# Moving the query pass behind the key and value passes, and writing the last round of a Strassen down-projection in a fixed order on all engines

## The chip, the cores and the metric

The kernel runs on one core of one Trainium2 chip. The metric is the device time of one execution in microseconds; the median of several executions is compared.

## The reference

The input x has 2048 tokens of 1024 values. All arithmetic is fp32.

```python
xn = _layernorm(x)
q, k, v = split_heads(xn @ wqkv)               # 32 heads of 32
phi(p) = concat(softmax(p), softmax(-p))       # p = q @ w_phi or k @ w_phi, per head
kv = einsum("bhsf,bhsd->bhfd", phi(pk), v);  z = sum over s of phi(pk)
s = (phi(pq) @ kv / (phi(pq) @ z + 1e-6)) @ wo
gate, up = xn @ w1, xn @ w3                    # 1024 -> 3584
g = silu((silu(gate) * up) @ w2)               # 3584 -> 1024
return x + s * g
```

## The kernel before, in words

Every large product is one level of a Strassen-like scheme with seven products (`ORDER`): operand sums are formed by VectorE, each fp32 operand is split into a high and a low fp32r part (`split`: a cast on ScalarE, a subtraction on VectorE), and three matmuls (`PASSES`) stand for one. The seven results go to three PSUM banks `a`, `b` and `c`. A bank takes several of the products one after another, so a product that adds to a bank waits until the bank's earlier value has been copied out. The stages run in this order.

1. **Gate and up** (`gate_up`, matmuls at L598): it leaves the hidden values in `h_d` in HBM, and the split operands of later stages in `xo_d`, `wkv_d` and `w2_d`.
2. **Three passes over the tokens** (loop `for c in range(3)` at L977). A pass takes eight pairs of token tiles; a pair is a block of seven products of twelve matmuls. Before the change, pass 0 is the query pass (`query_heads`, matmuls at L858), passes 1 and 2 are the key and value passes for the two halves of the heads (`heads`, L794, with the small `kv` products at L779). Each block loads the next pair's seven operands (`reload`, L563), 512 KB each. During a pass the next pass's seven weight operands of 2 MB are fetched (`fetch`, L167). The key and value passes split `wo` too (`wo_split`). The last pass also loads the first down operands (`load_b`).
3. **Query features** (`query_features`): of each of the four 128x512 quarters of a block, VectorE takes maximum and minimum (L837, L838), GpSimd, or VectorE for the last quarter, subtracts them (L839, L840), ScalarE takes the exponential (L842), and ScalarE's queue issues the DMA to `e_d` (L847). The quarters stand in two rooms of a pool `rw` with two buffers. Before, both rooms were taken once (`e_rooms`): room 0 had quarters (0,0) and (0,1), room 1 had (1,1) and (1,0). The quarters become ready in the order (0,0), (1,1), (0,1), (1,0), after the products A12, S3, S4 and A22. The key pass takes its rooms from the same pool (`room_ev`).
4. **Down** (`product`, L1135): seven rounds `kb` of eight pairs `i`, in steps. A step does three products of a new pair (`FIRST`) and four of the pair before, six matmuls each (`TURN`). `a_first` and `a_second` load the hidden values of a pair and prepare them; ScalarE, GpSimd and VectorE add results to 16 slabs in SBUF. In the last round finished slabs go through `gate` (Silu, L1035, and a store to `g_d`, L1036), and become the place of the attention's features. `load_kvz` and `load_e` (L1077) bring in what the attention needs, and `pieces` holds the first three tiles' normalisation (`z_products` on GpSimd, `z_sums` on VectorE, `weigh`, a small matmul in `add_pairs`, `invert`, `factors`, `scale`, `turn_e`), each at a pair and a place in the step.
5. **Attention and output** (from L1228): for each of 16 token tiles, `attend` (L1251), two halves of 24 matmuls (`out_half`, L1266), `gated` and a store. The weights come by `load_wo` (L1030), the gates by `load_g` (L1237).

Where `in_order(...)` names engines, their instructions stand in the order in which the code writes them; otherwise a scheduler puts each engine's instructions in an order of its own. Before, down's rounds leave all engines to the scheduler from step 6 on, and from the last half step on (`new is None`) SP, ScalarE, VectorE and GpSimd follow the written order. SP issues all DMAs but those to `e_d`, in order, and holds the ones behind a DMA that has to wait. A new DMA takes one of eight semaphores and waits until that semaphore's last DMA has landed.

## Time and profile before

| | us |
|---|---|
| median of 3 runs (lowest, highest) | 2419.08 (2416.06, 2419.09) |
| the profiled execution's own time | 2423.55 |
| its span from first to last instruction | 2421.8 |
| TensorE busy in the span | 2366.6 |
| VectorE, ScalarE, GpSimd busy | 1770.9, 856.9, 253.4 |

The busy time of TensorE counts its matmuls from start to end, and they overlap, so a busy share near one says little. What counts here is the distance from one matmul's start to the next, and the places where it grows. The mean granted clock of TensorE is 0.994 of full speed.

### The profile page before, as it was taken

To read this page: it belongs to the slowest core of one execution; us is meant where nothing else is said; L and a number is where in the kernel's file an instruction comes from. 1 tells how busy PE (TensorE), PEld (TensorE's weight loads), DVE (VectorE), ACT (ScalarE), POOL (GpSimd) and SP (SyncE) were. 2 spreads that over 40 slices of the span, in tenths; PEclk is the share of its full clock that TensorE was granted. 3 is DMA by queue.
4 is the path that set the end of the run, shared out by engine and by line. 5 is a ranking of instruction groups with operands and counts; after the bars stand their busy time and mean duration, and the time that the engine had idled before them with its cause. 6 is when DMAs were issued, how large, how long until landed. Compare 5 with 4: busy or idle time off the path is not lost.

```text
span 2421.8 us, 37223 instructions
## 1 busy us (share of the span) xinstructions
PE 2366.6 (98%) x14354; PEld 1941.1 (80%) x14354; DVE 1770.9 (73%) x2779; ACT 856.9 (35%) x1501; POOL 253.4 (10%) x249
## 2 busy tenths in 40 slices
PE   7999999999999999999998999999999999988999
PEld 6888888888888888888777888888888888766887
DVE  8877787765688888864676666666678888785775
ACT  6445454443455455442222222224322222231000
POOL 1000000000000000000331000000011111133662
PEclk9999999999999999999999999999999999999999
DMA  5446799976887988756999868855443244459773
GB/s 211 148 161 207 249 351 337 328 251 206 285 291 273 313 275 309 265 215 239 373 354 340 307 216 327 291 165 208 174 174 137 99 174 181 128 167 296 198 206 118
DMA packets 290001, 578.00 MB, mean 239 GB/s; under 512 B 24464, under 2 KB 140320, under 8 KB 287136
## 3 DMA queue, kind: packets, MB, share of 16 engines
q1 hardware_dynamic: 285216, 558.85, 67.8%
q10 hardware_dynamic: 4608, 16.78, 1.7%
q8 instruction: 113, 1.85, 0.3%
q14 instruction: 64, 0.52, 0.1%
HBM read 370.54 MB, written 205.00 MB: 238 GB/s over the span
## 4 chain that ended last, share of the span: by engine, by line
PE 46%; DMA 4%; DVE 1%; ACT 0%; issue 0%; SPq 0%; ACTq 0%
PE bankb L1135 12%; PE bankb L794 7%; PE pm L1266 7%; PE bankc L1135 6%; PE bankc L794 4%; PE banka L1135 3%; PE bankb L858 2%; PE banka L794 2%; DMA xoS<-xo_d1S 2%; PE bankc L858 1%; PE pkv L779 1%; PE po L1251 1%; DMA acc<-e_d 1%; DMA g_d<-acc 1%; PE banka L858 0%; DMA wos<-wo_d 0%
## 5 line engine op out<-in xcount | busy, mean ns | idle before, releaser
L93 DVE TENSOR_TENSOR bo<-rw,bo 128x512 fp32r<-128x512 f32 x336 | 230.9, 689 | 158.0 <-ACT bo L92 155.3
L92 ACT CAST bo<-rw 128x512 fp32r<-128x512 f32 x336 | 206.5, 617 | 12.9 <-DMA w_d2B<-w2o 3.1
L1135 PE MATMUL bankb<-bo,as 128*128 128x512 f32 x816 | 200.9, 389 | 0.0
L1135 PEld LDWEIGHTS bankb<-bo,as 128*128 128x128 f32 x816 | 153.2, 188 | 31.8
L598 PE MATMUL bankb<-op0S,bo 128*128 128x512 f32 x672 | 163.0, 391 | 1.9 <-ACT op0S L92 1.2
L598 PE MATMUL bankc<-op0S,bo 128*128 128x512 f32 x672 | 162.5, 391 | 0.3 <-DVE op0S L93 0.3
L598 PE MATMUL bankb<-op1S,bo 128*128 128x512 f32 x672 | 161.4, 389 | 0.9 <-ACT u L633 0.9
L598 PE MATMUL bankc<-op1S,bo 128*128 128x512 f32 x672 | 161.5, 389 | 0.0
L598 PE MATMUL bankb<-op0A,bo 128*128 128x512 f32 x672 | 159.7, 391 | 0.8 <-DVE bo L93 0.5
L598 PE MATMUL bankb<-op1A,bo 128*128 128x512 f32 x672 | 157.7, 390 | 0.0
L839 POOL TENSOR_TENSOR eq<-q,mm 128x512 f32<-128x512 f32 x24 | 25.3, 1052 | 1209.7 <-DVE mm L837 1113.7
L1135 PE MATMUL bankc<-bo,as 128*128 128x512 f32 x576 | 148.9, 393 | 1.5 <-ACT as L92 1.2
L1266 PE MATMUL pm<-wos,oT 128*128 128x512 f32 x576 | 141.5, 398 | 8.9 <-DVE oT L1257 6.0
L598 PEld LDWEIGHTS bankb<-op0S,bo 128*128 128x128 f32 x672 | 125.2, 188 | 28.5 <-ACT op0S L92 1.6
L598 PEld LDWEIGHTS bankb<-op1S,bo 128*128 128x128 f32 x672 | 126.0, 188 | 27.5 <-ACT u L633 1.3
L598 PEld LDWEIGHTS bankb<-op1A,bo 128*128 128x128 f32 x672 | 125.9, 188 | 27.4 <-DVE u L641 1.3
L598 PEld LDWEIGHTS bankc<-op1S,bo 128*128 128x128 f32 x672 | 126.1, 188 | 26.5 <-DVE bo L93 0.3
L598 PEld LDWEIGHTS bankb<-op0A,bo 128*128 128x128 f32 x672 | 125.2, 188 | 26.9 <-DVE bo L93 0.8
L598 PEld LDWEIGHTS bankc<-op0S,bo 128*128 128x128 f32 x672 | 125.3, 188 | 26.3 <-DVE op0S L93 0.7
L1266 PEld LDWEIGHTS pm<-wos,oT 128*128 128x128 f32 x576 | 108.0, 190 | 34.8 <-DVE oT L1257 6.8
L1135 PEld LDWEIGHTS bankc<-bo,as 128*128 128x128 f32 x576 | 108.4, 189 | 26.0 <-ACT as L92 2.2
L1147 DVE TENSOR_TENSOR acc<-bankb,acc 128x512 f32<-128x512 f32 x152 | 104.1, 686 | 26.7 <-PE bankb L1135 19.3
(249 smaller groups left out, 4412.6 us busy)
## 6 DMA issues: line engine op xcount, KB each, us to landing
rw<-in_w SPq DMA_DIRECT2D x112, 512.0 KB, 4.5
hr<-h_d SPq DMA_DIRECT2D x56, 512.0 KB, 3.6
h_d<-h SPq DMA_DIRECT2D x111, 256.0 KB, 4.9
xoS<-xo_d0S SPq DMA_DIRECT2D x44, 512.0 KB, 5.6
xoS<-xo_d1S SPq DMA_DIRECT2D x44, 512.0 KB, 5.2
xoA<-xo_d0A SPq DMA_DIRECT2D x33, 512.0 KB, 5.9
xoA<-xo_d1A SPq DMA_DIRECT2D x33, 512.0 KB, 5.4
e_d<-eq ACTq DMA_DIRECT2D x32, 512.0 KB, 7.7
```

The costliest lines, as they stand in the source:

```text
L92: nc.scalar.copy(hi, src)
L93: (by or nc.vector).tensor_sub(lo, src, hi.bitcast(F))
L598: nc.tensor.matmul(bank[b], bos[tb, f][bn][:, w, k], ao[an][:, u, k], start=first and n == 0, stop=LAST[b] == an and n == 11, skip_group_c ...
L779: nc.tensor.matmul(pkv[sl, m], e[:, m // 4, (m % 4) * P + 32 * h:(m % 4) * P + 32 * h + 32], v[:, 4 * (m % 4) + h], start=first and m == 0 ...
L794: nc.tensor.matmul(bank[b], xo[an][:, u, k], wb[bn][:, w, k], start=an in ("A11", "A12", "S1") and n == 0, stop=LAST[b] == an and n == 11, ...
L839: eng.tensor_sub(e[:, 0], p3, mm[:, 0, :].unsqueeze(2).to_broadcast([P, 16, DH]))
L858: nc.tensor.matmul(bank[b], xo[an][:, u, k], wb[bn][:, w, k], start=an in ("A11", "A12", "S1") and n == 0, stop=LAST[b] == an and n == 11, ...
L1135: nc.tensor.matmul(bank[b], t[:, u, pos + k], bos[kb, bn, k][:, w], start=first and n == 0, stop=LAST[b] == an and n == 5, skip_group_chec ...
L1147: nc.vector.tensor_add(c, pb, c)
L1251: nc.tensor.matmul(po[32 * j:32 * j + 32, a, 64 * k:64 * k + 64], kvs[sl, j, c, k], et[sl, :, 4 * k + j], start=True, stop=True, skip_grou ...
L1266: nc.tensor.matmul(p, oTs[t, h][:, a, k], wos[c, 4 * h + k][:, b], start=n == 0, stop=n == 3 * ND - 1)
```

## The change

The query pass becomes the third pass. Pass 0 and 1 are the key and value passes of the two halves, and the pending `kv` product and the first stores of `kv_out` move into the query pass's first block. The two rooms are no longer held for the whole pass. Each block takes an "early" room for quarters (0,0) and (1,1), and a "late" room for (0,1) and (1,0), from the same pool of two buffers.

In down's last round all five engines follow the written order from the round's first pair on. The operand preparation is cut into parts that stand between the products (`first_parts`, `second_parts`), the hidden values are loaded two pairs ahead, a pair's two gates come two steps after its first products instead of one, one in the middle of each half of the step, and the pieces of the normalisation have new places. The first tile's features get two ring slots of their own (`e0`) instead of slabs, and are loaded at the round's start. The order in which pairs use the slabs changes, and so do the places at which `wo` is loaded.

```diff
-            nc.sync.dma_start(t.bitcast(F), wkv_d[m - 2][n])
+            nc.sync.dma_start(t.bitcast(F), wkv_d[(1, 2, 0)[m - 2]][n])
...
+        def e_room():
+            return rwp.tile([P, 2, D], F, name="eq", tag="rw")
...
             elif an == "A12":
                 nc.vector.tensor_add(q00, pb, q00)
-                query_features(i, 0, 0, q00, rho, nc.gpsimd)
+                early = e_room()
+                query_features(i, 0, 0, q00, rho, nc.gpsimd, early[:, 0])
             elif an == "S3":
                 nc.vector.tensor_add(q11, pb, q11)
-                query_features(i, 1, 1, q11, rho, nc.gpsimd)
+                query_features(i, 1, 1, q11, rho, nc.gpsimd, early[:, 1])
             elif an == "S4":
                 nc.vector.tensor_add(q01, pb, q01)
-                query_features(i, 0, 1, q01, rho, nc.gpsimd)
+                late = e_room()
+                query_features(i, 0, 1, q01, rho, nc.gpsimd, late[:, 0])
             else:
-                query_features(i, 1, 0, pb, rho, nc.vector)
+                query_features(i, 1, 0, pb, rho, nc.vector, late[:, 1])
...
+            if an == "S1" and first:
+                kv(*pend)
+                out_now.extend(kv_out(1, pkv))
...
-            if c:
-                pend = heads(pos == 0, end, xo, wb, steps(), pend)
+            if last:
+                query_heads(i, pos == 0, xo, wb, steps())
             else:
-                query_heads(i, xo, wb, steps())
+                pend = heads(pos == 0, end, xo, wb, steps(), pend)
...
     pieces = {
-        (3, 0): [lambda: z_products(0)],
...
-        (8, 0): [lambda: z_sums(2, 1)],
+        (1, 5): [lambda: z_products(0)],
+        (2, 5): [lambda: z_sums(0, 0)],
+        (2, 6): [lambda: z_sums(0, 1), lambda: weigh(0)],
+        (3, 0): [lambda: add_pairs(0, "kv")],
...
+        (6, 6): [lambda: z_sums(1, 1), lambda: weigh(1)],
+        (7, 0): [lambda: add_pairs(1, "kv")],
...
+        (8, 6): [lambda: z_sums(2, 1)],
     }
...
-        if new is None:
-            in_order(ENG.SP, ENG.Activation, ENG.DVE, ENG.Pool)
+        elif end and i == 0:
+            in_order(ENG.SP, ENG.PE, ENG.Activation, ENG.DVE, ENG.Pool)
...
+            if end:
+                if m < 3 and new:
+                    then = next(gen2)
+                if m in (3, 4) and i < 7:
+                    first = next(gen1)
+                if m in (1, 4) and 1 < i:
+                    gate(i - 2, m // 4)
+                for do in pieces.get((i, m), ()):
+                    do()
...
-                for k in range(2, 8):
+                for k in range(6):
                     load_wo(k)
...
-    gate(len(pairs) - 1)
-    in_order(ENG.SP, ENG.PE, ENG.DVE, ENG.Pool, ENG.Activation)
...
     load_g(0)
     for c in range(2):
         attend(0, c)()
+    for j in range(2):
+        gate(len(pairs) - 1, j)
```

More of the change, by code (lines that the diff above doesn't have):

```diff
@@ L829, in heads, with query_features @@
         return pkv, False, last, e1, v1
-    def query_features(i, j, c, p, rho, eng):
-        e = e_rooms[j][:, c].rearrange("p (s h f) -> p s h f", s=2, f=DH)
+    def query_features(i, j, c, p, rho, eng, ef):
+        e = ef.rearrange("p (s h f) -> p s h f", s=2, f=DH)
         mm = small.tile([P, 2, 16], F, name="mm2")
@@ L840, in query_features @@
         eng.tensor_sub(e[:, 1], mm[:, 1, :].unsqueeze(2).to_broadcast([P, 16, DH]), p3)
-        ef = e_rooms[j][:, c]
         nc.scalar.activation(ef, ef, AF.Exp)
@@ L847, in query_features, with query_heads @@
         nc.scalar.dma_start(e_d[pairs[i][j]][:, c], ef)
-    def query_heads(i, xo, wb, steps):
+    def query_heads(i, first, xo, wb, steps):
         bank, rho = {}, small.tile([P, 2, 2, 16], F, name="rho")
+        def e_room():
+            return rwp.tile([P, 2, D], F, name="eq", tag="rw")
         for b, an, bn in ORDER:
@@ L884, in query_heads @@
                                   rho.rearrange("p j c h -> p j (c h)"))
+            if an == "S1" and first:
+                kv(*pend)
+                out_now.extend(kv_out(1, pkv))
             next(steps)
+            if out_now and not first:
+                out_now.pop()()
     def kv_out(c, pkv):
@@ L930, in load_b, with load_h @@
             bos[kb, n, kk] = t
-    def a_first(kb, i):
+    def load_h(kb, i):
         hq = quad("hr", F)
@@ L937, in a_first, with first_parts @@
                           h_d[i // 4][kb][i % 4].rearrange("p b h k t -> p (b h k t)"))
+        return hq
+    def first_parts(hq):
         hr = hq.rearrange("p b (h k) t -> p b h k t", h=2)
@@ L942, in a_first, with second_parts @@
         split(f1[:, 0], f1[:, 1], hq[:, 0])
+        yield
         split(f2[:, 0], f2[:, 1], sm)
-        return hq, sm, {"A11": (f1, 0), "A12": (f1, 2), "S2": (f2, 0)}
-    def a_second(hq, sm, _):
+        yield hq, sm, {"A11": (f1, 0), "A12": (f1, 2), "S2": (f2, 0)}
+    def second_parts(hq, sm, _):
         hr = hq.rearrange("p b (h k) t -> p b h k t", h=2)
+        t1, t2 = quad("as"), quad("as")
+        split(t1[:, 0], t1[:, 1], hq[:, 1])
+        yield
         s34 = work.tile([P, 4, P], F, name="s34", tag="w")
@@ L950, in a_second, with a_first @@
         nc.vector.tensor_sub(s34[:, 2:4], hr[:, 0, 1], sm)
-        t1, t2 = quad("as"), quad("as")
-        split(t1[:, 0], t1[:, 1], hq[:, 1])
+        yield
         split(t2[:, 0], t2[:, 1], s34)
-        return {"S1": (t1, 0), "A22": (t1, 2), "S3": (t2, 0), "S4": (t2, 2)}
+        yield {"S1": (t1, 0), "A22": (t1, 2), "S3": (t2, 0), "S4": (t2, 2)}
+    def a_first(kb, i):
+        return list(first_parts(load_h(kb, i)))[-1]
+    def a_second(*parts):
+        return list(second_parts(*parts))[-1]
     for d, b, t in hs:
@@ L962, in tile_kernel @@
     ready = []
-    e_rooms = [rwp.tile([P, 2, D], F, name="eq", tag="rw") for _ in range(2)]
     def wo_split(c, k, j, halves):
@@ L988, in steps @@
                 for j in range(7):
-                    if c:
-                        wo_split(c - 1, pos, j, halves)
+                    if not last:
+                        wo_split(c, pos, j, halves)
                     if j == 0:
@@ L1003, in steps @@
                     yield
-            if c:
+            if last:
+                query_heads(i, pos == 0, xo, wb, steps())
+            else:
                 pend = heads(pos == 0, end, xo, wb, steps(), pend)
-            else:
-                query_heads(i, xo, wb, steps())
             xo = xo if end else nxt
@@ L1016, in tile_kernel @@
     slabs = accp.tile([P, 16, D], F, name="acc")
-    SLABS = ((12, 13), (14, 15), (0, 1), (2, 3), (8, 9), (10, 11), (4, 5), (6, 7))
+    SLABS = ((0, 1), (14, 15), (8, 9), (10, 11), (2, 3), (4, 5), (6, 7), (12, 13))
     def acc_of(i):
@@ L1031, in load_wo, with gate @@
         wos[k // 8, k % 8] = t
-    def gate(i):
-        for m, t in zip(SLABS[i], pairs[i]):
-            nc.scalar.activation(slabs[:, m], slabs[:, m], AF.Silu)
-            nc.sync.dma_start(g_d[t], slabs[:, m])
+    def gate(i, j):
+        m = SLABS[i][j]
+        nc.scalar.activation(slabs[:, m], slabs[:, m], AF.Silu)
+        nc.sync.dma_start(g_d[pairs[i][j]], slabs[:, m])
     def slot_f(name):
@@ L1042, in load_kvz @@
     def load_kvz():
+        e0 = [slot_f("e0") for _ in range(2)]
         zb, kvs, w, own = (slot_f(name) for name in ("zb", "kvs", "rho", "own"))
@@ L1060, in load_kvz, with e_slab @@
         ezs.extend(slot_f("ez") for _ in range(2))
-        return (zb, kvs.rearrange("p (j c g d) -> p j c g d", j=4, c=2, g=4),
+        return (e0, zb, kvs.rearrange("p (j c g d) -> p j c g d", j=4, c=2, g=4),
                 w.rearrange("p (t g c h) -> p t c g h", t=NT, g=2, c=2), own)
-    def e_slab(t):
-        m = (12, 14, 8, 10)[t % 4]
-        return slabs[:, m:m + 2]
+    def e_slab(t, c):
+        return slabs[:, (12, 14, 8, 10)[t % 4] + c] if t else e0[c]
     def et_slab(t, c):
@@ L1076, in load_e @@
                 sl = slice(64 * a + 32 * s, 64 * a + 32 * s + 32)
-                nc.sync.dma_start(e_slab(t)[sl].rearrange("i c (g n) -> i c g n", g=2),
-                                  e_d[t][64 * a:64 * a + 64, :, s * 512:s * 512 + 512].rearrange("(g i) c n -> i c g n", g=2))
+                src = e_d[t][64 * a:64 * a + 64, :, s * 512:s * 512 + 512].rearrange("(g i) c n -> i c g n", g=2)
+                if t:
+                    m = (12, 14, 8, 10)[t % 4]
+                    nc.sync.dma_start(slabs[sl, m:m + 2].rearrange("i c (g n) -> i c g n", g=2), src)
+                else:
+                    for c in range(2):
+                        nc.sync.dma_start(e0[c][sl].rearrange("i (g n) -> i g n", g=2), src[:, c])
     def col(m):
@@ L1088, in z_products @@
             for c in range(2):
-                e = e_slab(t)[:, c].rearrange("p (g n) -> p g n", g=2)
+                e = e_slab(t, c).rearrange("p (g n) -> p g n", g=2)
                 nc.gpsimd.tensor_mul(ezs[c].rearrange("p (g n) -> p g n", g=2), e,
@@ L1116, in scale @@
         if t < NT:
-            e3 = e_slab(t)[:, c].rearrange("p (n f) -> p n f", f=DH)
+            e3 = e_slab(t, c).rearrange("p (n f) -> p n f", f=DH)
             nc.vector.tensor_mul(e3, e3, col(0)[:, 32 * c:32 * c + 32].unsqueeze(2).to_broadcast([P, H, DH]))
@@ L1121, in turn_e @@
         if t < NT:
-            nc.vector.transpose(et_slab(t, c), e_slab(t)[:, c])
+            nc.vector.transpose(et_slab(t, c), e_slab(t, c))
     def product(kb, i, bank, r, ao, b, an, bn):
@@ L1153, in tile_kernel @@
     pieces = {
-        (3, 0): [lambda: z_products(0)],
-        (3, 3): [lambda: z_sums(0, 0)],
-        (3, 5): [lambda: z_sums(0, 1), lambda: weigh(0), lambda: add_pairs(0, "kv")],
-        (4, 0): [lambda: invert(0), lambda: factors(0)],
-        (4, 1): [lambda: scale(0, 0), lambda: z_products(1)],
-        (4, 4): [lambda: scale(0, 1)],
-        (4, 6): [lambda: turn_e(0, 0)],
-        (5, 2): [lambda: turn_e(0, 1)],
-        (5, 4): [lambda: z_sums(1, 0)],
-        (6, 0): [lambda: z_sums(1, 1), lambda: weigh(1), lambda: add_pairs(1, "kv")],
-        (6, 3): [lambda: invert(1), lambda: factors(1), lambda: z_products(2)],
-        (7, 2): [lambda: z_sums(2, 0)],
-        (8, 0): [lambda: z_sums(2, 1)],
+        (1, 5): [lambda: z_products(0)],
+        (2, 5): [lambda: z_sums(0, 0)],
+        (2, 6): [lambda: z_sums(0, 1), lambda: weigh(0)],
+        (3, 0): [lambda: add_pairs(0, "kv")],
+        (3, 1): [lambda: invert(0), lambda: factors(0)],
+        (3, 5): [lambda: scale(0, 0)],
+        (3, 6): [lambda: scale(0, 1)],
+        (4, 5): [lambda: turn_e(0, 0)],
+        (4, 6): [lambda: turn_e(0, 1)],
+        (5, 5): [lambda: z_products(1)],
+        (6, 5): [lambda: z_sums(1, 0)],
+        (6, 6): [lambda: z_sums(1, 1), lambda: weigh(1)],
+        (7, 0): [lambda: add_pairs(1, "kv")],
+        (7, 1): [lambda: invert(1), lambda: factors(1)],
+        (7, 5): [lambda: z_products(2)],
+        (8, 4): [lambda: z_sums(2, 0)],
+        (8, 6): [lambda: z_sums(2, 1)],
     }
     old, banks, first, second = None, {}, ready[0], None
+    ahead = {}
     for r, new in enumerate(steps):
-        kb, i = new or (NKB, 0)
-        end = kb == NKB - 1
+        kb, i = new or (NKB, 8)
+        end = kb >= NKB - 1
         if r == 0:
@@ L1180, in tile_kernel @@
         parts = first
-        if r + 1 < len(steps) - 1:
+        if end:
+            if i < 6:
+                ahead[i + 2] = load_h(kb, i + 2)
+            if i == 0:
+                e0, zb, kvs, w_all, own = load_kvz()
+                xrs += [slot_f("xr") for _ in range(2)]
+                load_e(0)
+            elif 3 < i < 7:
+                load_e(i - 3)
+            if new:
+                gen2 = second_parts(*parts)
+            if i < 7:
+                gen1 = first_parts(ahead.pop(i + 1))
+        elif r + 1 < len(steps) - 1:
             first = a_first(*steps[r + 1])
+            if (kb, i) == (NKB - 2, len(pairs) - 1):
+                ahead[1] = load_h(NKB - 1, 1)
         bank = {}
         for m, (b, an, bn) in enumerate(TURN):
-            if kb >= NKB - 1:
-                for do in pieces.get((i if new else 8, m), ()):
-                    do()
             if an in FIRST:
@@ L1193, in tile_kernel @@
                 if new is None:
-                    for k in range(2 + 2 * BNAMES.index(bn), 4 + 2 * BNAMES.index(bn)):
+                    for k in range(6 + 2 * (BNAMES.index(bn) - 3), 8 + 2 * (BNAMES.index(bn) - 3)):
                         load_wo(k)
+            if end:
+                if m < 3 and new:
[6 more added lines that the diff above has]
+                    do()
         if new:
-            second = a_second(*parts) if r else ready[1]
-        if out_now and r:
-            out_now.pop()()
+            if end:
+                second = then
+            else:
+                second = a_second(*parts) if r else ready[1]
         if r == 1:
-            kv(*pend)
-            out_now += kv_out(1, pkv)
             late_rw += [rwp.tile([P, 2, 2, 512], R, name="late", tag="rw") for _ in range(2)]
@@ L1211, in tile_kernel @@
                 load_b(kb + 1, 6)
-        if end:
-            if i:
-                gate(i - 1)
-            if i == 0:
-                zb, kvs, w_all, own = load_kvz()
-                xrs += [slot_f("xr") for _ in range(2)]
-                for k in range(2):
-                    load_wo(k)
-            elif i in (1, 2, 5, 6):
-                load_e({1: 0, 2: 1, 5: 2, 6: 3}[i])
         old, banks = new, bank
+    for k in range(14, 16):
+        load_wo(k)
     close("ps")
     ps = pool("ps4", 3, space=PSUM)
-    gate(len(pairs) - 1)
-    in_order(ENG.SP, ENG.PE, ENG.DVE, ENG.Pool, ENG.Activation)
     oTs, gs = {}, {}
```

## The prediction

> **What bounds the kernel now.** I read the page's head first, then the chain of waits.

> ```profile
> span 2421.8 us, 37223 instructions
> ...
> PE 2366.6 (98%) x14354; PEld 1941.1 (80%) x14354; DVE 1770.9 (73%) x2779; ACT 856.9 (35%) x1501; POOL 253.4 (10%) x249
> ```

> The second line has each engine's busy time, its share and its instructions. TensorE is nearly always busy and no other engine is close, so the time is the number of matmuls, which the change leaves alone, plus the gaps between them. To find gaps I need the gapless duration. The timeline at the end of the query pass gives it:

> ```profile
> 1288.73 1.05 POOL L839 TENSOR_TENSOR eq<-q,mm 128x512 f32<-128x512 f32 x1 [6.02 <-issue]
> ...
> 1291.01 2.88 PE L858 MATMUL bankb<-op2T,xoS 128*128 128x512 f32 x12
> 1293.73 2.88 PE L858 MATMUL bankc<-op2B,xoS 128*128 128x512 f32 x12
> ...
> 1298.73 0.33 ACTq L847 DMA_DIRECT2D e_d<-eq  x1
> ```

> Twelve matmuls run 2.88 us, but the next product starts 2.72 us after (1293.73 - 1291.01): 0.227 a matmul. A block of seven products is 19.05 us; a down step of seven products of six, 9.52. Now the stages' ends, from the source view of each matmul line (first and last start):

> ```profile
> L858 PE MATMUL bankb<-op2B,xoA x96: 387/389/504, 1135.2 to 1282.6; 128*128 128x512 f32 x96
> ...
> L794 PE MATMUL bankb<-op3B,xoA x96: 388/389/500, 1299.2 to 1457.3; 128*128 128x512 f32 x96
> L794 PE MATMUL bankb<-op4B,xoA x96: 389/389/497, 1475.6 to 1624.5; 128*128 128x512 f32 x96
> L1135 PE MATMUL bankb<-bo,af x288: 387/389/628, 1642.8 to 2180.3; 128*128 128x512 f32 x144
> ```

> The query pass takes 1299.2 - 1135.2 = 164.0 against 8 x 19.05 = 152.4: 11.6 lost. The key passes do the same work as each other, but the first takes 176.4 and the second 167.2: 9.2 lost. Where, the timeline says:

> ```profile
> 1156.26 4.58 PE L858 MATMUL bankb<-op2T,xoA 128*128 128x512 f32 x12 [4.41 <-DMA xoA<-xo_d0A]
> 1233.89 0.33 ACTq L847 DMA_DIRECT2D e_d<-eq  x1
> 1234.90 4.59 PE L858 MATMUL bankc<-op2B,xoS 128*128 128x512 f32 x12 [2.37 <-ACT q L864]
> 1315.99 0.69 DVE L112 TENSOR_TENSOR ev<-k,mm 128x512 f32<-128x512 f32 x1 [7.58 <-DMA e_d<-eq]
> 1316.67 4.86 PE L794 MATMUL bankb<-op3T,xoS 128*128 128x512 f32 x12 [6.46 <-ACT ev L807]
> ```

> Each idle stretch is followed by slow matmuls (4.58 for 2.88: 1.7 more). The first waits for an operand behind fetched weights: 4.41 + 1.7 and some 0.5 of small gaps, 6.6. The second waits for a copy that stands on ScalarE's queue behind an `e_d` issue: 2.37 + 1.7 = 4.1. The last, at the turn to the key pass, waits until the final `e_d` store has freed its room: 6.46 + 2.0, and smaller gaps. Busy time by stretch, with DMA share and GB/s at the end:

> ```profile
> 1135.00:1299.00 164.00, 157.05 (x674) 127.92 (x673) 112.75 (x189) 47.59 (x56) 48.48 (x47) 0.98 0.97 364
> 1299.00:1476.00 177.00, 169.27 (x1636) 136.47 (x1635) 108.02 (x153) 35.94 (x49) 3.51 (x19) 0.98 0.81 288
> 1476.00:1640.00 164.00, 163.90 (x1625) 132.81 (x1624) 108.67 (x155) 40.05 (x58) 1.95 (x15) 1.00 0.73 249
> 2095.00:2194.00 99.00, 88.75 (x367) 69.34 (x365) 72.15 (x114) 34.58 (x51) 31.87 (x29) 0.97 0.64 189
> ```

> The query pass has its DMA engines 97% busy, the third pass 73%. Now the last round:

> ```profile
> 2095.48 1.52 PE L1135 MATMUL bankc<-bo,as 128*128 128x512 f32 x6
> ...
> 2136.42 2.41 POOL L1090 TENSOR_TENSOR ez<-acc,zb 128x1024 f32<-128x1024 f32 x1
> ...
> 2138.86 1.22 DVE L1095 TENSOR_REDUCE own<-ez 128x32 f32<-128x1024 f32 x1 [0.86 <-POOL ez L1090]
> ...
> 2140.54 0.43 PE L1105 MATMUL us<-own 128*128 128x64 f32 x2 [1.68 <-POOL own L1100]
> ...
> 2194.05 1.71 PE L1251 MATMUL po<-acc,kvs 64*32 64x64 f32 x128
> ```

> 2194.05 - 2095.48 = 98.57 for eight steps and four products, 8 x 9.52 + 5.44 = 81.6: 17.0 lost. After it, with E = 2194.05:

> ```profile
> 2197.45 4.01 SPq L1030 DMA_DIRECT2D late<-wo_d  x4
> ...
> 2207.28 0.32 SPq L1237 DMA_DIRECT2D g<-g_d  x1
> 2219.19 0.69 DVE L1274 TENSOR_TENSOR g<-pm,g 128x512 f32<-128x512 f32 x1 [16.91 <-DMA g<-g_d]
> 2220.94 4.51 PE L1266 MATMUL pm<-wos,oT 128*128 128x512 f32 x10 [5.98 <-DVE oT L1257]
> ```

> VectorE waits 16.91 for the first gate and the second tile's features queue behind it: the second tile's output starts at E + 26.9. Its work before that is 2.4 (attention's start) + 2 x 24 x 0.227 + 1.8 for two attention parts and one sum: about E + 15, 12 lost. So 11.6 + 9.2 + 17.0 + 12 = about 50 us is the most that can be gained.

> **The change part by part.** *First pass, now keys.* It still starts with a backlog of stores and 2 MB weights, so the 6.6 stays but for the 0.5 MB `e_d` stores ahead of the late operand: at 364 GB/s one is 1.4. I take 5.5, between 3.5 and 8.5: above 6.6 because ScalarE now has to cast `wo` pieces behind a load in the same backlog.

> *Query in third place.* The turn from queries to keys is gone, and with it the 9.2. The pass keeps reload (25.7 MB), `e_d` (16.8), down operands and hidden values (some 6): 48 MB in 152 us, 320 GB/s, where it now has 364 and waits. The fetches move to the other passes, which then carry what pass 1 has now, 288.

> The rooms are the new cost. An early room is written again by the next block's (0,0), whose subtraction starts at 1288.73 in its block, 19.05 later in the next, and its (1,1) leaves at 1298.73. So there are 1288.73 + 19.05 - 1298.73 = 9.05 us to land. The tile view of `e_d` and the copies that ScalarE has behind that quarter's exponential say what is there:

> ```profile
> DMA to landing us min/median/max: 3.7/7.6/13.1
> ...
> 1292.28 0.59 ACT L864 COPY q<-bankc 128x512 f32<-128x512 f32 x1 [0.40 <-ACT eq L842]
> ```

> That copy ends at 1292.87 and frees the bank that the product at 1293.73 takes: 0.86 of slack. TensorE waits only for a landing over 9.9. The median of 7.6 was measured at 97% DMA share, and the share falls, so I take 1.5 for the pass, 0 to 6. Late rooms have the same spacing and no bank behind them.

> *Turn from queries to down.* SP's `rho_d` store waits for the last sum and holds a hidden-value load behind it. The store is some 10.6 into the step, the load is needed two steps on: 1, 0 to 4. The passes gain 11.6 + 9.2 - 5.5 - 1.5 - 1 = 12.8.

> *Last round.* Preparation and loads a step ahead take away waits on operands. A written order brings its own: at (3,0) and (7,0) TensorE meets the small `us` product in its queue, right after the second `z_sums` (1.22) and GpSimd's 0.32 for `weigh` have begun. At 2140.54 that cost 1.68; with half speed, as after the 2.37 at 1234.90, 1.7 more. I take 2 each and 1 elsewhere: 5 remain of 17.0, 2 to 9, a gain of 12. VectorE has 72.15 busy in the stretch, which becomes 72.15/81.6 = 88%: it fits, with little room. Queued behind VectorE's `z_sums` is the bank addition of the product before, so a late `ez` from GpSimd holds banks too; `z_products` stand a step ahead, 9.52 us for 2 x 2.41 of GpSimd's work (2136.42).

> The clock bears on this. After 2.37 idle, twelve matmuls took 4.59 for 2.88. [...]

> *Tail.* SP issues loads 1.23 apart (eight from 2197.45 to 2207.28, 9.83 us), each waiting for an earlier one to land. Now six pieces of `wo` start at about E - 7, and the first gate's load is the 19th from there, landing 2.5 past its turn: E - 7 + 19 x 1.23 + 2.5 = E + 18.9. With the 1.75 from 2219.19 to 2220.94, the second tile starts at E + 20.6: 6.3 gained of the 12, 3 to 10.

> *At nothing:* the `kv` product moves with its instructions, hidden under TensorE's own queue; the four more loads for `e0` have a step of 9.52 each in which SP is free; ScalarE's work is 34.58 of the 99. If that cover fails, each costs its wait once, below 2.

> Sum: 12.8 + 12 + 6.3 = 31.1. The profiled execution took 2423.55 (its span and 1.75 around it) and becomes 2392.5; the median of the runs, 2419.08, lies 4.5 below the profiled one, so the forecast is 2388. About 0.2%, 4.8 us, can be told from no change.

> **The rivals.** *Rooms wait.* If landings stay at 13.1, TensorE waits 13.1 - 9.9 = 3.2 and 1.7 of half speed in every second block (a wait lengthens the next gap): 4 x 4.9 = 19.6, 18.1 more than the 1.5 taken: 13 gained, 2406. For it: the maximum was reached. Against: the lighter pass.

> *Last round gains nothing* (the order only trades waits: VectorE at 88% falls behind and the loads stay at 1.23): 31.1 - 18.3 = 12.8 gained, 2406. With the rooms' waits too nothing is left: 5.3 lost, 2424.

> *Slower: ScalarE held by its `e_d` issues*, as at 1233.89, at 4.1 each. The gain is gone from 31.1 / 4.1 = 8 such events, one a block; at 12 to 16, of 32 issues, 49 to 66 go for the 31.1: 2437 to 2454. For it: ScalarE has no other queue for them, and SP's hidden-value loads and `rho_d` stores take semaphores also. Against: one event cost time in eight blocks at a 97% share.

> *Better:* nearly all of the 50 go: some 43 gained, 2376.

> **How the numbers follow.** Forecast 0.54 (its own range 2379 to 2398, the ends of its terms combined as squares, 7, and a little for their being judged); rooms 0.11; no gain in the last round 0.13; both 0.04; ScalarE held 0.11; better 0.07. Faster is 0.54 + 0.11 + 0.13 + 0.07 = 0.85, same 0.03 and slower 0.11 + 0.01 (both together lies at the edge of what can be told). The range 2376 to 2410 leaves out the held case, both, and a little of the better one.

> **What would show it.** Right: key passes with no gap over 2 but in the first block; blocks of 19.05 in the query pass; gaps before `us` of about 2; the first gate landing near E + 19. Wrong: TensorE in the query pass idle for ScalarE's copies behind `eq` (rooms) or behind an issue to `e_d` (held), or a last round still above 93.

## The result, and the profile after

| | before | after |
|---|---|---|
| median of 4 runs (lowest, highest), us | 2417.57 (2415.56, 2419.09) | 2400.65 (2400.20, 2401.13) |
| the profiled execution and its span | 2423.55, 2421.8 | 2401.13, 2399.3 |

The ratio of the times is 0.9931, with a 95% interval of [0.9913, 0.9948]: the changed kernel is 16.9 us faster. The forecast was 2388 in a range of 2376 to 2410. The direction and the range held, but the gain is little more than half of the 29.6 to 31.1 that was worked out.

The head of the page after, and busy time by stretch (the two key passes, the query pass, the last round; PE, PEld, DVE, ACT, POOL, then the granted clock, the DMA share and GB/s):

```profile
span 2399.3 us, 37196 instructions
...
PE 2360.1 (98%) x14354; PEld 1938.1 (81%) x14354; DVE 1776.9 (74%) x2779; ACT 855.1 (36%) x1501; POOL 253.2 (11%) x249
```

```profile
1135.00:1306.00 171.00, 167.78 (x1604) 135.32 (x1603) 101.72 (x140) 35.73 (x49) 1.85 (x14) 0.99 0.84 310
1306.00:1474.00 168.00, 167.92 (x1750) 135.87 (x1737) 106.02 (x148) 35.64 (x50) 2.12 (x16) 1.00 0.81 282
1474.00:1630.00 156.00, 154.39 (x738) 126.50 (x738) 119.14 (x202) 48.91 (x61) 48.00 (x46) 1.00 0.90 326
2083.00:2177.00 94.00, 86.66 (x389) 69.55 (x395) 78.90 (x116) 34.43 (x52) 31.61 (x29) 0.96 0.59 181
```

The instruction counts of the engines are those of before. The query pass now has a DMA share of 0.90 where it had 0.97, and the granted clock is 1.00 in it. One number goes the wrong way: VectorE is busy for 78.90 us in the last round, with 116 instructions, where it had 72.15 with 114. The same instructions take longer there.

From the starts of the matmuls, in the two profiles:

| stage | before, us | after, us | change | forecast |
|---|---|---|---|---|
| three passes | 507.6 | 494.9 | -12.8 | -12.8 |
| down, first six rounds | 452.7 | 452.7 | 0 | 0 |
| down, last round | 98.6 | 94.2 | -4.4 | -12 |
| attention and output | 227.7 | 222.6 | -5.2 | -6.3 |

Down starts at 1629.9, its last round at 2082.59, and the attention (E) at 2176.80:

```profile
L1159 PE MATMUL bankb<-bo,af x288: 387/389/628, 1629.9 to 2164.2; 128*128 128x512 f32 x144
...
2082.59 1.52 PE L1159 MATMUL bankc<-bo,as 128*128 128x512 f32 x6
...
2176.80 0.86 PE L1286 MATMUL po<-acc,kvs 64*32 64x64 f32 x64
```

The stages' changes add up to 22.4 between the profiles. The medians differ by 16.9, because the profiled execution of before lay 6.0 above its four-run median and that of after only 0.5. So 8.7 us of the forecast are missing from the stages, nearly all from the last round, and the rest is the offset.

The last round after, in the timeline (TensorE's waits longer than 1 us and what followed two of them):

```profile
2116.41 0.43 PE L1129 MATMUL us<-own 128*128 128x64 f32 x2 [2.26 <-POOL own L1124]
2116.65 2.18 PE L1159 MATMUL bankb<-bo,af 128*128 128x512 f32 x6
2118.63 2.61 PE L1159 MATMUL bankb<-late,as 128*128 128x512 f32 x6
...
2147.22 2.09 PE L1159 MATMUL bankb<-bo,as 128*128 128x512 f32 x6 [2.84 <-DVE acc L1171]
2149.11 2.72 PE L1159 MATMUL bankc<-bo,as 128*128 128x512 f32 x6
...
2162.75 0.43 PE L1129 MATMUL us<-own 128*128 128x64 f32 x2 [1.38 <-POOL own L1124]
```

Six matmuls take 1.52 at full speed, here 2.61 and 2.72: half speed follows the first two waits. The two waits before `us` were forecast. The one at 2147 was not: TensorE waits for a bank that VectorE has not added up yet. What VectorE and GpSimd did just before it:

```profile
2139.69 1.29 POOL L1169 TENSOR_TENSOR acc<-acc,u 128x512 f32<-128x512 f32 x1 [8.08 <-ACT u L1168]
2139.78 1.76 DVE L93 TENSOR_TENSOR as<-hr,as 128x512 fp32r<-128x512 f32 x1
2140.95 5.33 POOL L1114 TENSOR_TENSOR ez<-acc,zb 128x1024 f32<-128x1024 f32 x2
2141.46 2.61 DVE L965 TENSOR_TENSOR s<-hr,sm 128x256 f32<-128x256 f32 x1
2144.00 2.56 DVE L966 TENSOR_TENSOR s<-hr,sm 128x256 f32<-128x256 f32 x1
2146.49 0.68 DVE L1171 TENSOR_TENSOR acc<-bankb,acc 128x512 f32<-128x512 f32 x1
```

The source view says what the stretched instruction takes elsewhere (shortest, median, longest in ns): 416 in the middle, 2612 here.

```profile
L965 DVE TENSOR_TENSOR s<-hr,sm x56: 407/416/2612, 1624.2 to 2163.3; 128x256 f32<-128x256 f32 x56
...
L1171 DVE TENSOR_TENSOR acc<-bankb,acc x152: 648/690/693, 1641.5 to 2177.3; 128x512 f32<-128x512 f32 x152
```

Eight of VectorE's subtractions on two SBUF operands are stretched by 0.5 us or more, and each ends 0.3 to 0.6 us behind the end of a GpSimd instruction: four behind a product with z (L1114), four behind an addition to `acc` (L1169). The additions from a PSUM bank (L1171) never stretch: their longest is 693 ns. Summed over the last round, VectorE's instructions last 11.2 us longer than their lines' medians, 7.4 of them behind the products and 3.8 behind the additions; in before it is 2.2. That is the theory that the experiments test: VectorE's instructions on such operands stand still while GpSimd computes, and the new order puts `z_products` beside VectorE's operand preparation.

### The profile page after: what moved, and what is told of

Its sections match the earlier page's. It is cut to its first block, busy times and chain, and to the rows that moved or that the text cites. A ratio compares the mean times of both kernels' runs of the same rounds, so it can differ in the third digit from the quotient of the medians.

```text
span 2399.3 us, 37196 instructions
## 1 busy us (share of the span) xinstructions
PE 2360.1 (98%) x14354; PEld 1938.1 (81%) x14354; DVE 1776.9 (74%) x2779; ACT 855.1 (36%) x1501; POOL 253.2 (11%) x249
## 5 line engine op out<-in xcount | busy, mean ns | idle before, releaser
L598 PEld LDWEIGHTS bankb<-op0A,bo 128*128 128x128 f32 x672 | 125.2, 188 | 26.9 <-DVE bo L93 0.8
L598 PEld LDWEIGHTS bankc<-op0S,bo 128*128 128x128 f32 x672 | 125.4, 188 | 25.7
L1171 DVE TENSOR_TENSOR acc<-bankb,acc 128x512 f32<-128x512 f32 x152 | 103.9, 685 | 21.1 <-PE bankb L1159 16.9
```

Of the source, the lines that this page charges most:

```text
L598: nc.tensor.matmul(bank[b], bos[tb, f][bn][:, w, k], ao[an][:, u, k], start=first and n == 0, stop=LAST[b] == an and n == 11, skip_group_c ...
L1171: nc.vector.tensor_add(c, pb, c)
```

## The experiments

Ratios are against runs of the kernel before on the same chip, with a 95% interval.

**1. The two halves of the change alone.** `passes_only` joins the new passes to the old last round and output; `down_only` joins the old passes to the new last round and output.

> This has the three passes of the kernel after and down's last round and output as before. Between the two profiles the passes shrank by 12.8 us (507.6 to 494.9), the last round by 4.4 (98.6 to 94.2) and the output by 5.2. Theory: the stages add up, so this kernel keeps the passes' part: its passes take about 495 us, its last round 98 to 99, and the time is 12.8 below the profiled execution of before, at 2410; against the median of before, 2417.6, that is 7.3 less, since the medians differ by 16.9 of which the last stages hold 9.6. Rival: the passes' gain depends on what follows (the first down operands, the late slots), and the time is 2417 or more.

> This has the passes as before, query first, and down's last round and output as after. Theory: the stages add up, so it gains 9.6 us (4.4 in the last round, 5.2 in the output), 2408, and its query pass still takes about 164 and its turn to the keys still waits. Rival: part of the last round's gain comes from the passes, and it gains less than 5.

Measured: 2409.75 us, ratio 0.9955 [0.9943, 0.9968], and 2410.46 us, ratio 0.9963 [0.9949, 0.9977]. The product of the ratios is 0.9918, against 0.9931 [0.9913, 0.9948] for the whole. In `passes_only` the passes take 494.0, the last round 98.9 and the output 225.9; in `down_only` 503.1, 94.8 and 223.1 (its query pass takes 160.2, where some 164 was expected; experiment 6 has the reason). The stages add up: each half gives about half of the gain. The old waits stand where the old part stands, first, in the timelines, the turn from queries to keys in `down_only`, then a cast behind Silu in `passes_only`:

```profile
1312.67 4.73 PE L794 MATMUL bankb<-op3T,xoS 128*128 128x512 f32 x12 [6.90 <-ACT ev L807]
```

```profile
2106.05 0.96 PE L1143 MATMUL bankb<-bo,af 128*128 128x512 f32 x2 [2.38 <-ACT af L92]
```

**2. The products with z on VectorE, and in pieces.** `z_vector` takes GpSimd out of the disputed place by giving VectorE more work, for the first three tiles; `z_pieces` leaves the work on GpSimd and cuts each product into eight short instructions.

```diff
-                nc.gpsimd.tensor_mul(ezs[c]...
+                (nc.vector if t < 3 else nc.gpsimd).tensor_mul(ezs[c]...
```

> The kernel after, but the products with z of the first three tiles are computed by VectorE in place of GpSimd, at the same places of the written order. In the last round of after, VectorE's instructions on two SBUF operands beside a running GpSimd instruction last as long as that one (as<-hr,as 1.76 for 0.68, s<-hr,sm 2.61 and 2.56 for 0.41): 11.2 us in all, against 2.2 in before. Theory (shared access): these instructions stand still while GpSimd computes; without GpSimd they return to 0.68 and 0.41, VectorE gets two products of some 1.3 a tile for 4 to 5.4 us of standing, and the wait of 2.84 at 2147 falls below 1; time 3 to 6 us lower, about 2396. Rival (VectorE too full): what makes TensorE wait is the amount of work in VectorE's written order; 2.7 us more at the same place make the wait at 2147 longer, to 4 or more, and the time 3 to 6 higher, about 2405.

> The kernel after, with each product with z of the first three tiles cut into eight instructions of 128 columns, still on GpSimd. Theory (shared access): a VectorE instruction on two SBUF operands then stands for one such piece, some 0.3 to 0.6, and goes on; the excess of VectorE's instructions in the last round falls from 11.2 to below 7, the wait of 2.84 at 2147 falls below 1.5, and the time is 2 to 4 lower. Rival (GpSimd's work is in the way as a whole): VectorE stands as long in all, piece after piece, and the time is that of after within 1.

Measured: `z_vector` 2397.41 us, ratio 0.9905 [0.9891, 0.9919]. Its last round takes 90.7 in place of 94.2, VectorE's excess falls from 11.2 to 4.0 (what is left stands behind GpSimd's additions to `acc`), and the wait at 2147 is gone although VectorE has more to do. The rival, that VectorE is simply too full there, had the wait grow. It is refuted for that wait. But VectorE is late elsewhere: the waits before `us` grow to 2.92 and 2.94.

```profile
2115.17 0.43 PE L1129 MATMUL us<-own 128*128 128x64 f32 x2 [2.92 <-POOL own L1124]
...
2158.33 0.43 PE L1129 MATMUL us<-own 128*128 128x64 f32 x2 [2.94 <-POOL own L1124]
```

`z_pieces`: 2398.79 us, ratio 0.9911 [0.9898, 0.9924], beside 2399.69 for after itself on that chip, ratio 0.9920 [0.9907, 0.9932]; the two cannot be told apart, so by the time alone it is the rival's outcome that came. Its profile does show the theory's step: the excess falls from 11.7 to 6.2, the stretched subtractions take 0.68, about one piece's length (two pieces take 1.52), and the wait at 2147 is gone. The last round takes 90.1 for 93.1, though the wait at the second `us` grows to 3.17, and the output 223.1 for 222.2.

```profile
2138.61 1.52 POOL L1117 TENSOR_TENSOR ez<-acc,zb 128x128 f32<-128x128 f32 x2
...
2139.13 0.68 DVE L965 TENSOR_TENSOR s<-hr,sm 128x256 f32<-128x256 f32 x1
```

**3. `us` two products later, and both edits.**

```diff
-        (3, 0): [lambda: add_pairs(0, "kv")],
-        (3, 1): [lambda: invert(0), lambda: factors(0)],
+        (3, 2): [lambda: add_pairs(0, "kv")],
+        (3, 3): [lambda: invert(0), lambda: factors(0)],
...
```

> The kernel after, but the small us product of tiles 0 and 1, and what follows it, stand two products later: (3,2) and (7,2) in place of (3,0) and (7,0). Theory: TensorE's waits of 2.26 and 1.38 before us, and 1.7 of half speed behind the first, are caused by the place of us in TensorE's own order, so they go: 5 us lower, 2395 to 2396. Rival: they only show that VectorE is behind, and TensorE waits for a bank one or two products on instead: under 1.5 us lower.

> The kernel after, unchanged, on the chip on which the next three run. It gives the reference for them: 2399 to 2402 is expected, as in its four runs so far (2400.2 to 2401.1), with last round 94.2, output 222.6 and passes 494.9 in its profile.

> Both edits to after at once: products with z on VectorE, and us two products later. Alone they took the last round from 94.2 to 90.7 and 87.8, and the output from 222.6 to 222.7 and 224.8. Theory A (two separate causes): all four waits go, the last round comes to 83 to 85, near its gapless 81.6, and the time is 7 to 9 below after, about 2393. Theory B (the output is held by the loads of wo and of the first gates, not by the end of the round): the round comes to 83 to 85 as well, but the output grows to 227 or more, and the time is no lower than with us alone, about 2396.

Measured: `us_later` 2396.74 us, ratio 0.9901 [0.9886, 0.9916]; the last round takes 87.8. Both waits before `us` are gone, the one for VectorE's bank stays, at 3.00:

```profile
2143.83 1.66 PE L1159 MATMUL bankb<-bo,as 128*128 128x512 f32 x6 [3.00 <-DVE acc L1171]
```

`after_again` 2399.69 us, last round 93.1. `z_us`, on the same chip, 2392.51 us, ratio 0.9887 [0.9874, 0.9899]: 7.2 below after. Its last round takes 84.3 of a gapless 81.6, so the two causes are separate and hold 8.8 of the 11.5 us that `after_again` lost there. What TensorE still waits before `us` is 0.2:

```profile
2115.64 0.43 PE L1129 MATMUL us<-own 128*128 128x64 f32 x2 [0.19 <-POOL own L1124]
```

Theory B was right for a small part: the output grew from 222.2 to 223.9, 1.7 of the 8.8. On a third chip the same kernel, `z_us_again`, had 2390.36 us, ratio 0.9875 [0.9861, 0.9889]. It is the fastest version here.

> z_us unchanged, on the chip of the two others, as their reference: 2391.5 to 2393.6 as before.

**4. The rooms grouped by token tile.**

```diff
-                early = e_room()
-                query_features(i, 0, 0, q00, rho, nc.gpsimd, early[:, 0])
+                top = e_room()
+                query_features(i, 0, 0, q00, rho, nc.gpsimd, top[:, 0])
...
-                query_features(i, 1, 1, q11, rho, nc.gpsimd, early[:, 1])
+                low = e_room()
+                query_features(i, 1, 1, q11, rho, nc.gpsimd, low[:, 1])
...
```

> The kernel after, but a block's two rooms are grouped by token tile, (0,0) with (0,1) and (1,1) with (1,0), as the kernel before grouped them, in place of by time. A room is then written again by the next block's (0,0) while its (0,1) left only some 5.5 us earlier (against 9.05), and TensorE waits for a landing over about 6.4 in place of 9.9. In after the landings were 2.6/6.1/9.5 us (lowest, median, highest), so none there reached 9.9. Theory (rooms set the query pass): it waits in most blocks, one to three us each with half speed behind the longer ones, and the time is 8 to 20 higher, 2408 to 2420. Rival (the landings are no limit): within 2 of after.

Measured: 2403.34 us, ratio 0.9930 [0.9918, 0.9942], 3.7 above `after_again`; the passes take 499.0 for 493.7. The chain that the prediction drew is in the timeline: GpSimd waits for a landing of `e_d`, its subtraction ends late, the exponential and the copy behind it come late, and TensorE waits 3.23, with half speed behind it (4.61 for 2.88).

```profile
1525.02 1.05 POOL L839 TENSOR_TENSOR eq<-q,mm 128x512 f32<-128x512 f32 x1 [10.33 <-DMA e_d<-eq]
...
1527.11 1.06 ACT L841 ACTIVATE eq<-eq 128x1024 f32<-128x1024 f32 x1 [5.96 <-POOL eq L840]
...
1528.56 0.59 ACT L867 COPY q<-bankc 128x512 f32<-128x512 f32 x1 [0.40 <-ACT eq L841]
1529.20 4.61 PE L861 MATMUL bankc<-op4B,xoS 128*128 128x512 f32 x12 [3.23 <-ACT q L867]
```

It happens in two of the eight blocks (1.28 in the other), not in most, so the effect is real and smaller than the 8 to 20 expected. The quarter that holds the room there is (0,1): two of its stores landed later than 6.4 us, after 8.9 and 7.9, just ahead of the two waits, and the four others that a next block has to wait for, and whose landing is known, took 2.6 to 5.4.

**5. The gates at the end of the step, and the last gates behind the loads.** `gates_at_end` puts after's gates where before had them. `z_us_gates` starts from `z_us`.

```diff
-                if m in (1, 4) and 1 < i:
-                    gate(i - 2, m // 4)
+                if m == 6 and 0 < i < 8:
+                    for j in range(2):
+                        gate(i - 1, j)
```

> The kernel after, but a pair's two gates (Silu and store) come at the end of the step after its first products, as in the kernel before, in place of one pair later and in the middle of the two halves. Theory: ScalarE, in order, then waits for VectorE's last bank addition of the step and computes 2 us of Silu before the casts that the next products need, as in before, where TensorE waited 2.38 for af behind Silu at 2117: the last round grows from 94.2 (93.1 in its second profile) by 3 to 8, the time to 2403 to 2408. Rival: the casts are for products a step ahead, so the round stays within 1; the stores leave earlier, and the output may get up to 2.5 shorter: 2397 to 2400.

> z_us, but the gates of pair 6 (two Silu and two stores of 512 KB) come behind the loads of wo and of the first gate, next to those of pair 7, in place of between the loads of wo. Theory (the start of the output is held by transfers at 1.23 each): the loads of wo behind them and the first gate land up to 2.5 earlier, and the output takes 221.5 to 222.5 in place of 223.9: 1.5 to 2.5 lower, 2390 to 2391. Rival: the two stores only move ahead of the features of tile 4 and of the next gates, which then come late: within 0.5 of z_us, 2392.5.

Measured: `gates_at_end` 2408.09 us, ratio 0.9947 [0.9933, 0.9961]; the last round takes 100.6, 6.4 to 7.5 more than after. That is what the old order took, 98.6 and 101.1 in two profiles: without the later gates the written order gains nothing in this round. The wait did not come where I had put it: TensorE does not wait for a cast. ScalarE's cast stands behind two Silu (the second line), VectorE waits 1.03 for it and then reaches `z_sums` later, and the wait before `us` grows from 2.26 to 3.97 and from 1.38 to 4.00.

```profile
2104.55 2.07 ACT L1054 ACTIVATE acc<-acc 128x1024 f32<-128x1024 f32 x2
2106.52 0.60 ACT L92 CAST as<-hr 128x512 fp32r<-128x512 f32 x1
...
2107.16 0.69 DVE L93 TENSOR_TENSOR as<-hr,as 128x512 fp32r<-128x512 f32 x1 [1.03 <-ACT as L92]
```

`z_us_gates` 2395.50 us, ratio 0.9894 [0.9879, 0.9910], beside 2390.36 for `z_us_again`: a miss. The first gate does land earlier, and the second tile's output starts 19.8 us after the round's end (2189.66 - 2169.89) in place of 23.1. But the output takes 225.3 for 223.3. TensorE, earlier at the next tile, waits there for the second gate, and then for `us`:

```profile
2189.66 5.29 PE L1301 MATMUL pm<-wos,oT 128*128 128x512 f32 x22 [2.22 <-DVE oT L1292]
...
2205.69 5.32 PE L1301 MATMUL pm<-wos,oT 128*128 128x512 f32 x22 [1.69 <-DVE oT L1292]
2213.45 0.43 PE L1129 MATMUL us<-own 128*128 128x64 f32 x2 [2.44 <-POOL own L1124]
```

The second gate landed 34 us after the round's end in both kernels. SP, in order, holds its load behind tile 4's features (2196.75 behind 2194.20 in `z_us_gates`, 2192.79 behind 2190.24 in `z_us_again`), and those behind the last gate's store (issued by 2183.82 and by 2180.57). Of the 6.7 us between the two spans, 2.0 are the output's and 1.0 the passes'. The other 3.6 are one wait in gate and up, where the kernels do not differ, for an operand whose weights landed late (VectorE waits 5.02 for them, 2.18 in `z_us_again`), with half speed behind it:

```profile
607.88 4.38 PE L598 MATMUL bankb<-op1A,bo 128*128 128x512 f32 x11 [2.09 <-DVE bo L93]
```

Five of the fourteen profiles have a wait of 1.0 to 2.1 at this place, `z_us` one of 2.10 without half speed, the others none over 0.4: it varies from one execution to the next. So 1.4 to 2.0 us, against the two profiles of `z_us`, go with the gates, as the rival had it but at a higher price; for the rest of the 5.1 between the medians this is not shown.

**6. A second profile of the kernel before.**

> The kernel before, unchanged, for a second profile. The prediction took over that its first profiled execution was 4.5 us above the median. Theory: that execution had a wait which others lack, the one at 1234.90 (2.37 idle and 1.7 of half speed, for a copy behind an issue to e_d); without it the passes take 503 to 504 in place of 507.6, as in the run with down's part alone (503.1), while last round (98.6) and output (227.7) stay within 1, and the time is 2417 to 2420. Rival: the passes are 507 to 508 again, and the difference lies elsewhere.

Measured: 2420.31 us. The passes take 505.1, the last round 101.1, the output 225.5. The wait at 1234.90 is there, but short:

```profile
1232.49 3.02 PE L858 MATMUL bankc<-op2B,xoS 128*128 128x512 f32 x12 [0.93 <-ACT q L864]
```

So it explains some 3 us of the first profile, and the last round and the output moved by 2.5 up and 2.3 down. The expectation was right in its place and wrong that nothing else varies. The runs of before spread over 2415.6 to 2427.9 on all chips, those of after over 2398.1 to 2403.7. In the two profiles of before, the waits that differ most (2.37 and 0.93 at the copy; 2.57 and 4.50 in the last round, at 2155.11 and 2153.80) are among those that the change removes; that this holds for the other executions is not shown.

## Why the prediction was right, and where it was not

**The passes: right, and to the tenth by luck.** 12.8 was forecast and 12.8 came.

```profile
L794 PE MATMUL bankb<-op2B,xoA x96: 389/389/499, 1135.0 to 1288.1; 128*128 128x512 f32 x96
...
L794 PE MATMUL bankb<-op3B,xoA x96: 389/389/499, 1306.4 to 1455.6; 128*128 128x512 f32 x96
```

```profile
L861 PE MATMUL bankb<-op4B,xoA x96: 389/389/499, 1473.8 to 1610.8; 128*128 128x512 f32 x96
```

The key passes take 171.4 and 167.4, the query pass 1473.8 to 1629.9, 156.1. So the first key pass lost 4.0 against the second, where 5.5 was taken, and the query pass lost 3.7 over 152.4, where 1.5 and 1 were taken for pass and turn: two errors of over 1 us that cancel. Of the 3.7, 0.8 are the `kv` product, put at nothing, which TensorE computes in the first block. The query pass's three waits, 0.4 to 0.7 each, are all in the last block, where down's first operands are prepared beside the features. The rooms' own limit of 9.9 us was not reached. In the query pass (1474 to 1645) the stores' landings were

```profile
DMA to landing us min/median/max: 2.6/6.1/8.2
```

and the maximum, 13.1 before, fell while the DMA share fell from 0.97 to 0.90, as the first rival's counterargument had it. The view from which the prediction took 7.6 and 13.1 also counts the loads of `e_d` in later stages; for the stores alone the median is 7.7 and the maximum the same, so its use of them holds; the 9.5 that is named for after in experiment 4 is a load of the output too. The longest wait of TensorE for a copy by ScalarE in the query pass is 0.70, so the slower rival did not occur.

**The last round: the step that failed.** It took 94.2, and by the prediction's own sign, a last round above 93, this part was wrong. 5 us of waits were to remain, 2 to 9 at the ends; 12.6 remained. `us` cost 2.26 and 1.38 idle, near the 2 each, and 1.7 of half speed behind the first, which was kept for the range's end. "Elsewhere" was 6 to 7 in place of 1: VectorE's 72.15 was counted at durations that held in the order of before, and the new order stretched them by 9 us beside GpSimd, so a bank came late at 2147, which cost 2.84 and 1.7 of half speed. That the work "fits, with little room" was not the error by itself: in `z_us` VectorE is busy for 77.52 of the round's 84.31 us, and TensorE waits there nowhere longer than 0.81.

```profile
2082.63:2166.94 84.31, 83.09 (x366) 67.61 (x364) 77.52 (x122) 34.79 (x52) 16.10 (x23) 1.00 0.64 199
```

So VectorE did fall behind, as the rival of the last round had it, but because its instructions were stretched, and not for the 88% alone; 7.6 of the 12 us that this rival took away were lost. A row that could have warned was in the trace of before, where the second of the two subtractions (L966 in after) has a median of 418 ns and a longest of 1516:

```profile
L950 DVE TENSOR_TENSOR s<-hr,sm x56: 360/418/1516, 1632.3 to 2176.8; 128x256 f32<-128x256 f32 x56
```

Which operands it takes, the traces show: in after a subtraction on two SBUF operands (2141.46) took 2.61 us for 0.42 beside a GpSimd product of 2.84, in `z_pieces` 0.68 beside two pieces of 1.52 together, and in after the additions from a PSUM bank at 2098.07 and 2100.88 took 0.68 each beside two products of 5.44 together. I had not weighed that row.

**The output: right in its mechanism, and 1.1 short.** The load of the first gate was issued at 2187.01 and VectorE had it at 2197.20, E + 20.4 with E = 2176.80; E + 18.9 was forecast. The second tile started at E + 22.2, forecast 20.6, and the output took 5.2 us less, forecast 6.3.

```profile
2187.01 0.32 SPq L1272 DMA_DIRECT2D g<-g_d  x1
...
2197.20 0.69 DVE L1309 TENSOR_TENSOR g<-pm,g 128x512 f32<-128x512 f32 x1 [12.36 <-DMA g<-g_d]
```

**The offset: carried over wrongly.** The forecast subtracted the 4.5 by which the profile of before exceeded its median from the forecast for after as well. After's profile lies 0.5 above its own median: 4.0 of the 12.7 us between 2388 and 2400.65. Profile 22.4 against 31.1, and median 16.9 against 31.1, are therefore different errors.

## What to carry to other kernels

Before an operation is placed beside another engine's work, look at the shortest, median and longest durations of its line: a longest several times the median can mean that the other engine's work stretches it, as here (2612 ns for 416 beside GpSimd), and busy time counted in the old order then need not hold in the new one. In a written order a small dependent instruction on the bottleneck engine should not stand right behind its producer: two products (2.7 us) later its wait here was 0.2. The two causes are best mended together, since with the products moved alone the waits before `us` grew to 2.92 and 2.94. Time saved ahead of a stage that begins with a wait for a transfer was in part lost there (1.7 of 8.8 us in `z_us`), so the next stage belongs in the sum.

## What the runs showed of the hardware that was not expected

The same wait does not always cost the same. Before the first `us` TensorE waited 2.26 in after and ran at half speed behind it (six matmuls in 2.61). In the second profile of the same kernel it waited 2.28 and did not:

```profile
2115.45 0.44 PE L1129 MATMUL us<-own 128*128 128x64 f32 x2 [2.28 <-POOL own L1124]
2115.70 1.63 PE L1159 MATMUL bankb<-bo,af 128*128 128x512 f32 x6
2117.17 1.54 PE L1159 MATMUL bankb<-late,as 128*128 128x512 f32 x6
```

In the last rounds with the new order there are 13 lone waits between 2.2 and 3.3 us: behind 8 of them half speed cost 1.5 to 1.7 us more, behind 5 some 0.1. The granted clock shows what sets them apart. But for the one in which a profile ends, its half-speed stretches last 3.41 us, or twice that, and within a profile their starts lie whole multiples of 3.413 us apart: in after three of them are 1154.96, 2117.51 and 2148.24, which is 282 and 9 times. In the second profile of after one starts at 2144.44, which is 9 times behind 2113.72. Laid over the waits, this grid of stretches gives, for the first `us` in after (the first two rows) and in its second profile (the last two):

```profile
2114.10:2117.51 3.41, 1.15 (x7) 0.97 (x7) 3.41 (x7) 0.00 (x0) 0.32 (x1) 1.00 0.60 203
2117.51:2120.92 3.41, 3.41 (x10) 2.63 (x9) 0.78 (x2) 1.99 (x4) 1.33 (x2) 0.50 0.00 0
...
2113.72:2117.13 3.41, 1.68 (x8) 1.46 (x9) 3.41 (x7) 0.00 (x0) 0.32 (x1) 1.00 0.46 154
2117.13:2120.54 3.41, 3.41 (x16) 2.80 (x15) 1.94 (x4) 2.57 (x4) 1.57 (x2) 1.00 0.22 92
```
